# A fused attention and feed-forward kernel: each engine's issue order taken from a table in the source, in place of priorities and hand-set order

## Chip, cores and metric

The kernel runs on one core of one Trainium2 chip. The metric is the time of one execution on the device in microseconds (us); lower is better. The core has five instruction streams that run beside each other: TensorE (PE in the profile), VectorE (DVE), ScalarE (ACT), GpSimd (POOL) and SyncE (SP), which here only issues transfers. Each stream runs its instructions in the order in which they stand in it, and an instruction starts when what it waits for is done.

## The reference

Batch 4, 8 heads, 576 positions, head width 64, with a bias on the scores from a small network on the distance of two positions; then a feed-forward layer over 2304 tokens (model width 512, hidden width 2048).

```python
scores = q @ k.T / sqrt(64)
x      = log1p(|i - j|) / log1p(max(i, 1))          # one number for each pair of positions
bias   = relu(x * w1 + b1) @ w2                     # 32 hidden units, one value for each head
attn   = softmax(scores + bias)
a      = attn @ v                                   # heads side by side: 2304 x 512
h      = a @ w_in
g      = h * clip(h + 3, 0, 6) / 6
out    = g @ w_out
```

`w_in` and `w_out` arrive as 64-bit numbers (two 32-bit words each), and most products are made of three matmuls on 16-bit high and low parts (high by high, high by low, low by high).

## The kernel before

**Stages.** (1) The bias table: for 36 groups of 16 positions a hidden layer (`z_e` on DVE, `z_a` or `z_e` on ACT), a matmul (`b_ps`), an eviction with scale (`bo`, line 932 on ACT) and a store to DRAM. The attention tiles read the table back as `bt` or, for a tile that is used often, `k` (line 500, on SP). (2) `w_in` comes in 8 chunks of 1 MB: a load (line 248 on SP, into `w`), absolute value (258 on ACT), sign (259 on POOL), three DVE passes that put the two words together and take the row maximum (266, 269, 272), then a power-of-two scale of the row (210, 165, 215) and a split into a 16-bit high half (129 on ACT) and low half (146 on DVE, `wi`). Lines 266 to 272 write into the space of `wo`, the later home of `w_out`, so the first `w_out` loads can't start until the last low halves of `w_in` have been read from there. (3) `w_out` goes the same way in 8 chunks `cu`, staged in `wo` or `z_e`; the low halves are again line 146, into `wo`. The maximum over all its rows (line 152 `m_w`, a matmul `m_ps` on PE, line 161 `p_w`, then 220 and 222) gives `r_w2c`, with which the first hidden tiles `g` are scaled on DVE (line 127) before the first output matmul may read them. (4) `v_scale`: the maximum of |v| of each batch, from loads `va` or `vf` (line 179, SP) and a DVE reduction each (181). (5) 144 attention tiles: scores `s_ps` on PE, bias and row maximum on DVE (571, 750 ns each), the exponential on ACT (582), transposes `t_ps`, and the product with v `pv_ps`. (6) The feed-forward of each half batch: `h_ps` (line 793, PE), activation on ACT (783, 770), DVE (776) and POOL (772), `o_ps` (line 816, PE).

**What sets the order.** The program is traced by Python generators: the attention tiles go on one by one, and between them run steps of the weight preparation, the bias table and the feed-forward, at rates from a table of settings (`rw1`, `ro`, `rf` and others). A scheduler then places the traced instructions by a simulated timeline and by priorities (`ahead`, `low`, `ranked`, with offsets such as `a_bo` -100). Three things bind it further. `behind(k)` wraps many loads so that each comes after a bias load that was noted in `bias_loads` (an order without a wait). `keep_order("PE")` in `open_steady` switches to the traced order on PE from tile 37 on, and `keep_order("SP")` does so for SP from tile 45 on.

Of the kernel before, what the change touches and what calls it, by code (L numbers as in the profile page):

```python
# [13 lines left out]
U32 = mybir.dt.uint32  # L14
# [16 lines left out]
F64_BIAS = 2.0 ** -112  # L31
F64_MAX = float(np.uint32(0x0FEFFFFF).view(np.float32))


@with_exitstack
def attention_moe_kernel(
# [17 lines left out]
    nc = tc.nc  # L54
# [173 lines left out]

    bias_loads = []

    def behind(k=-1):

        return tc.issue_after(bias_loads[k]) if len(bias_loads) > max(k, 0) else nullcontext()

    def pick(name, k):
        return cfg[name][k % len(cfg[name])]

    def f64_load(src, k=None):

# [7 lines left out]
        with behind(cfg["wb"]) if k is not None else nullcontext():  # L247
            dq("w").dma_start(out=t, in_=src.bitcast(U32))
        return t
# [140 lines left out]
    def load_direct(b, p):  # L390

        t = qk_p.tile([128, 512 + S], F32, tag="hi", name="qk0")
        with behind():
            dq("q").dma_start(out=t, in_=qkd[b, p])
        qk_t[b, p, 0] = t
# [5 lines left out]
    def load_qk(b, p, u):  # L401
        w = S + QW[u]
        t = st_p.tile([128, 1024], F32, tag="st", name="st")[:, 0:w]
        with behind():
            dq("k").dma_start(out=t, in_=qk[b, p][:, 256 * u:256 * u + w])
        st_t[b, p, u] = t
# [34 lines left out]
    def load_v(b, p, u):  # L441
# [4 lines left out]
        else:  # L446
            t = st_p.tile([128, VC], F32, tag="vs", bufs=2, name="vs")
        with behind():
            dq("v").dma_start(out=t, in_=vp[b, p])
        v_t[b, p, u] = t  # L450
# [24 lines left out]
    def load_bias(b, p, i):  # L475
# [22 lines left out]
        else:  # L498
# [3 lines left out]
            )  # L502
        bias_loads.append(d.ins)
        return out, src
# [685 lines left out]
    HOLD, LAST = cfg['hold'], NT + 5  # L1190
    in_order = ctx.enter_context(ExitStack())

    def keep_order(*names):
        engines = {getattr(mybir.EngineType, e) for e in names}
        in_order.enter_context(tc.manual_schedule(engines=engines))


# [28 lines left out]
    def open_steady():  # L1226
# [8 lines left out]
        steady[0] = True  # L1235
        keep_order("PE")

# [33 lines left out]
    for n in range(-1, NT + 7):  # L1271
# [33 lines left out]
    for q_ in queue:  # L1305
        drain(q_)
    in_order.close()

# [60 lines left out]
```

## Time and profile before

| what | value |
|---|---|
| time, median of 3 runs | 670.89 us (667.25, 670.89, 673.08) |
| profiled execution | 668.28 us, span of the core 666.3 us |
| mean granted TensorE clock | 0.982 of full |
| busy: PE, DVE, ACT, POOL | 631.3, 462.4, 503.0, 212.6 us |

The span runs from the first to the last instruction of the core; the profiled execution's own time has 2 us around it. Matmuls are pipelined and their ends are modelled, so a busy share of 95% says that PE had little idle time, not that every matmul ran at its best rate. Times in the rows are in us from the span's start unless marked ns.

### The profile page before, as it was taken

To read this page: it belongs to the slowest core of one execution; us is meant where nothing else is said; L and a number is where in the kernel's file an instruction comes from. 1 tells how busy PE (TensorE), PEld (TensorE's weight loads), DVE (VectorE), ACT (ScalarE), POOL (GpSimd) and SP (SyncE) were. 2 spreads that over 40 slices of the span, in tenths; PEclk is the share of its full clock that TensorE was granted. 3 is DMA by queue.
4 is the path that set the end of the run, shared out by engine and by line. 5 is a ranking of instruction groups with operands and counts; after the bars stand their busy time and mean duration, and the time that the engine had idled before them with its cause. 6 is when DMAs were issued, how large, how long until landed. Compare 5 with 4: busy or idle time off the path is not lost.

```text
span 666.3 us, 14803 instructions
## 1 busy us (share of the span) xinstructions
PE 631.3 (95%) x5440; PEld 451.8 (68%) x5440; DVE 462.4 (69%) x1116; ACT 503.0 (75%) x993; POOL 212.6 (32%) x267
## 2 busy tenths in 40 slices
PE   8677899887999899999999999999999999999997
PEld 3224556664777667788888887777777777777775
DVE  6798978899866987867678676776687657731310
ACT  7996777887859998888689778876888678832620
POOL 0211124766121531154135314531244125300410
PEclk9977999998899999999999999999999999999999
DMA  8798967744688989998999999798979996550000
GB/s 294 281 347 301 372 251 265 246 177 149 178 204 203 234 209 260 235 211 208 286 253 217 252 220 179 142 203 183 184 134 197 183 193 127 97 102 21 1 11 31
DMA packets 176649, 130.58 MB, mean 196 GB/s; under 512 B 138304, under 2 KB 145728, under 8 KB 175552
## 3 DMA queue, kind: packets, MB, share of 16 engines
q1 hardware_dynamic: 166784, 114.14, 69.8%
q10 hardware_dynamic: 9792, 15.49, 7.9%
q8 instruction: 43, 0.70, 0.4%
q14 instruction: 30, 0.25, 0.1%
HBM read 77.54 MB, written 15.49 MB: 140 GB/s over the span
## 4 chain that ended last, share of the span: by engine, by line
PE 72%; DVE 9%; DMA 7%; issue 4%; ACT 3%; POOL 1%; ACTq 0%; SPq 0%; DVEq 0%; POOLq 0%
PE o_ps L816 28%; PE h_ps L793 24%; PE s_ps L559 9%; PE pv_ps L724 7%; DMA wo<-in_w_out_dram 3%; DMA va<-in_vp_dram 2%; PE b_ps L893 2%; DMA w<-in_w_in_dram 2%; DVE bt L571 1%; DVE cu L269 1%; DVE wo L272 1%; DVE wo L269 1%; DVE cu L272 1%; DVE cu L266 1%; DVE vparts L181 1%
## 5 line engine op out<-in xcount | busy, mean ns | idle before, releaser
L793 PE MATMUL h_ps<-x,wi 128*128 128x256 f16 (+1 forms) x1536 | 199.8, 288 | 1.7 <-DVE p_v L161 1.7
L816 PE MATMUL o_ps<-g,wo 128*128 128x256 f16 (+1 forms) x1536 | 196.5, 286 | 0.0
L793 PEld LDWEIGHTS <-wi 128*128 128x128 f16 x1536 | 148.4, 99 | 49.6 <-issue 11.1
L816 PEld LDWEIGHTS <-wo 128*128 128x128 f16 x1536 | 146.9, 98 | 46.8 <-issue 9.3
L772 POOL TENSOR_TENSOR g<-t,g 128x256 f16<-128x256 f32 (+1 forms) x128 | 105.5, 834 | 191.8 <-ACT g L770 191.0
L582 ACT ACTIVATE bt<-bt,sm 128x576 f32<-128x576 f32 x144 | 110.7, 770 | 39.7 <-DVE sm L571 38.0
L146 DVE SCALAR_TENSOR_TENSOR hl<-bt,sm,hl 128x576 f16<-128x576 f32 x112 | 95.5, 868 | 24.2 <-ACT hl L129 22.3
L129 ACT ACTIVATE hl<-bt,sm 128x576 f16<-128x576 f32 x112 | 83.9, 766 | 4.8 <-ACT bt L582 3.3
L776 DVE SCALAR_TENSOR_TENSOR t<-t,t,h_ps 128x320 f32<-128x320 f32 (+1 forms) x112 | 57.0, 515 | 38.9 <-ACT t L783 38.0
L418 POOL TENSOR_TENSOR qkl<-st,qkh 128x576 fp32r<-128x576 f32 (+2 forms) x48 | 55.8, 1184 | 72.7 <-ACT qkh L411 67.9
L770 ACT ACTIVATE g<-t 128x256 f16<-128x256 f32 (+1 forms) x128 | 55.3, 438 | 22.5 <-DVE t L776 22.1
L783 ACT ACTIVATE t<-h_ps,t,hr 128x320 f32<-128x320 f32 (+1 forms) x112 | 64.8, 587 | 9.2 <-PE h_ps L793 6.8
L571 DVE CUSTOM_DVE_ANT_0 bt<-s_ps,bt 128x576 f32<-128x576 f32 x88 | 64.6, 750 | 5.9 <-PE s_ps L559 4.2
L590 DVE TENSOR_SCALAR sm<-sm 128x1 f32<-128x1 f32 x112 | 16.7, 151 | 42.5 <-ACT bt L582 42.4
L826 ACT ACTIVATE ot<-o_ps,os 128x256 f32<-128x256 f32 (+1 forms) x32 | 15.7, 491 | 37.2 <-PE o_ps L816 34.8
L932 ACT ACTIVATE bo<-b_ps,cv_sb,isc 128x576 f32<-128x576 f32 (+36 forms) x60 | 36.0, 637 | 2.2 <-PE b_ps L893 2.0
L872 DVE TENSOR_SCALAR z_e<-T,nbp 128x576 f32<-128x576 f32 (+17 forms) x76 | 33.1, 486 | 4.4 <-PE b_ps L893 2.4
L571 DVE CUSTOM_DVE_ANT_0 bt<-s_ps,k 128x576 f32<-128x576 f32 x40 | 28.7, 751 | 8.3 <-PE s_ps L559 6.1
L724 PE MATMUL pv_ps<-at,vh 128*64 128x320 f16 (+1 forms) x432 | 32.0, 293 | 0.0
L259 POOL TENSOR_SCALAR w<-w 128x1024 f32<-128x1024 f32 x8 | 10.1, 1260 | 67.1 <-ACT wo L258 59.2
L539 PE MATMUL s_ps<-qk 64*128 64x288 f32 x128 | 25.5, 476 | 5.9 <-DVE sm L571 4.4
L876 ACT ACTIVATE z_e<-T,bp 128x576 f32<-128x576 f32 (+17 forms) x36 | 24.5, 703 | 7.8 <-PE b_ps L893 3.5
(130 smaller groups left out, 835.7 us busy)
## 6 DMA issues: line engine op xcount, KB each, us to landing
bt<-bias SPq DMA_DIRECT2D x36, 576.0 KB, 5.5
w<-in_w_in_dram SPq DMA_DIRECT2D x8, 1024.0 KB, 7.4
vs<-in_vp_dram SPq DMA_DIRECT2D x24, 320.0 KB, 4.5
st<-in_qk_dram SPq DMA_DIRECT2D x16, 448.0 KB, 4.1
bias<-bo ACTq DMA_DIRECT2D x20, 295.5 KB, 4.7
wo<-in_w_out_dram SPq DMA_DIRECT2D x5, 1024.0 KB, 5.8
bias<-bo ACTq DMA_DIRECT2D x16, 288.0 KB, 5.9
bt<-bias SPq DMA_DIRECT2D x32, 144.0 KB, 3.4
```

Source lines behind the costliest of these rows:

```text
L129: nc.scalar.activation(out=out, in_=full, func=AF.Copy, scale=scale)
L146: nc.vector.scalar_tensor_tensor(out=out, in0=full, scalar=scale, in1=high, op0=ALU.mult, op1=ALU.subtract)
L418: nc.gpsimd.tensor_sub(out=lo[:, c:c + w], in0=t[:, c:c + w], in1=hi[:, c:c + w].bitcast(F32))
L559: nc.tensor.matmul(out=s_t[n + j][:, a, 0:HALF], lhsT=w[q], rhs=m[rows, cs], start=(k == 0), stop=(k == 2),)
L571: nc.vector.tensor_tensor_reduce(out=halves(bt), in0=ps, in1=halves(src), op0=ALU.add, op1=ALU.min, scale=-0.125, scalar=3.0e38, accum_out ...
L582: nc.scalar.activation(out=bt, in_=bt, func=AF.Exp, scale=-1.0, bias=sm[:, 0:1], accum_out=total)
L724: nc.tensor.matmul(out=ps[64 * s:64 * s + 64, 0:n], lhsT=w[:, 128 * c + 64 * s:128 * c + 64 * s + 64], rhs=at[:, c, s * n:(s + 1) * n], st ...
L772: e.tensor_sub(out=g[:, 1], in0=uu, in1=g[:, 0])
L776: nc.vector.scalar_tensor_tensor(out=t_t[f], in0=t_t[f], scalar=cols(f)[2], in1=h_t.pop(f)[:, 0:n], op0=ALU.min, op1=ALU.mult,)
L783: nc.scalar.activation(out=t_t[f], in_=h_t[f][:, 0:n], func=AF.Relu, scale=cols(f)[0], bias=cols(f)[1],)
L793: nc.tensor.matmul(out=h_t[f][:, 0:n], lhsT=wi[:, a, c, f * 128:(f + 1) * 128], rhs=x[:, e, c], start=(k == 0), stop=(k == 3 * KC - 1),)
L816: nc.tensor.matmul(out=ops[:, 0:n], lhsT=wo[:, a, f, e * 128:(e + 1) * 128], rhs=g_t[f][:, r], start=(f == 0 and a == 0 and r == 0), stop= ...
```

## The change

The instructions and the data they pass stay as they were. `behind`, `bias_loads` and `keep_order` go. A table `ISSUE` gives for each engine a permutation of its traced instructions: SP 116 entries, POOL 247, ACT 907, DVE 939, PE 1367 (instructions by the number at which they are traced; whatever comes behind the last entry follows in traced order). At the end of the program `issue_in_order` adds, along each engine's list, a dependency from each instruction to the one before it that has no semaphore: it binds the scheduler's order on that engine and adds no wait. The priorities stay in the code, and the chain leaves them nothing to choose.

```diff
+ISSUE = {
+    "SP": """
+0-1 3 2 15 4 7 18 5 8 20 10 23 22 6 11 9 25 12-14 17 31 16 19 21 26 24 27 33 30 28 35 29 47 32 34 36
...
+    "DVE": """
+8 3 5-6 17 14 0 7 15 9-10 16 19 18 4 47 20 11 21 62 22 53 24 64-65 25 23 26 29 31 30 32 27-28 35
...
+def issue_in_order(tc, nc):
+
+    traced = {}
+    for i in nc.cur_bb.bb.instructions:
+        if not i.opcode.startswith("Tile"):
+            traced.setdefault(i.engine.name, []).append(i)
+    after = mybir.DependencyInfo(mybir.DependencyClass.NoSync, mybir.DependencyReason.DATA)
+    for name, seq in traced.items():
+        order = []
+        for run in ISSUE[name].split():
+            lo, _, hi = run.partition("-")
+            order.extend(range(int(lo), int(hi or lo) + 1))
+        order.extend(range(len(order), len(seq)))
+        for a, b in zip(order, order[1:]):
+            tc.add_manual_dep(seq[b], seq[a].name, after, reason="order")
...
-            with behind():
-                dq("v").dma_start(out=t, in_=vp[b, p])
+            dq("v").dma_start(out=t, in_=vp[b, p])
...
-    bias_loads = []
-
-    def behind(k=-1):
-
-        return tc.issue_after(bias_loads[k]) if len(bias_loads) > max(k, 0) else nullcontext()
...
-        steady[0] = True
-        keep_order("PE")
+        steady[0] = True
...
-        if n == cfg["spn"]:
-            keep_order("SP")
...
-    in_order.close()
+    issue_in_order(tc, nc)
```

Against the order before, every engine's instructions stand in another order up to a point and in the same one from there: PE in its first 1366 of some 5000 matmuls, DVE and ACT up to the places that the trace of before has at 256 us and shortly after 250 us, SP in its first 115 transfers. Three places follow. Numbers behind a name tell the tiles of one name apart; "x3" stands for three alike in a row. Line numbers of the kernel after are higher by some 149 for the same code up to line 460 and by some 137 below.

DVE at the end of the `w_out` preparation, before: `L161` is `p_w`, `L222` is `r_w2c`, `L146` on `wo` a low half of a chunk, `L146` on `hl` a low half of an attention tile, `L872` the hidden layer of the bias table.

```order
L872 TENSOR_SCALAR z_e_114<-T_113,nbp_117 128x320 x3
L594 RECIPROCAL sm_1588<-sm_1588 128x1
L594 RECIPROCAL sm_1654<-sm_1654 128x1
L161 TENSOR_REDUCE p_w2_1697<-m_ps_1695 128x1
L146 SCALAR_TENSOR_TENSOR wo_96<-cu_1626,w2s_1058,wo_96 128x1024
L203 TENSOR_SCALAR os0_1773<-hs0_991,p_w2_1697 128x1
L203 TENSOR_SCALAR os1_2169<-hs1_2165,p_w2_1697 128x1
L220 RECIPROCAL rm_w2_1699<-p_w2_1697 128x1
L203 TENSOR_SCALAR os2_3369<-hs2_3365,p_w2_1697 128x1
L146 SCALAR_TENSOR_TENSOR hl_1672<-bt_1306,sm_1588,hl_1672 128x576
L146 SCALAR_TENSOR_TENSOR hl_1733<-bt_1306,sm_1654,hl_1733 128x576
L222 TENSOR_SCALAR r_w2c_1701<-w2p_1057,rm_w2_1699 128x8
```

The same place after (`L310` is 161, `L368` and `L370` are 220 and 222, `L413` is 272, `L1009` is 872, `L276` is 127):

```order
L310 TENSOR_REDUCE p_w2_1697<-m_ps_1695 128x1
L731 RECIPROCAL sm_1588<-sm_1588 128x1
L368 RECIPROCAL rm_w2_1699<-p_w2_1697 128x1
L370 TENSOR_SCALAR r_w2c_1701<-w2p_1057,rm_w2_1699 128x8
L413 SCALAR_TENSOR_TENSOR cu_1626<-z_e_114,cu_1626 128x1024
L1009 TENSOR_SCALAR z_e_114<-T_113,nbp_117 128x320 x2
L276 TENSOR_SCALAR g_1353<-g_1353,r_w2c_1701 128x2x256
L727 TENSOR_SCALAR sm_1654<-sm_1654 128x1
L1009 TENSOR_SCALAR z_e_114<-T_113,nbp_117 128x320
L731 RECIPROCAL sm_1654<-sm_1654 128x1
L295 SCALAR_TENSOR_TENSOR hl_1672<-bt_1306,sm_1588,hl_1672 128x576
```

The chain of the maximum has moved ahead of the last packing pass, the hidden layer, the two `hl` halves and the low halves of the last two chunks (`cu_1564` and `cu_1626`); those two low halves stand 16 and 19 rows below the end of this piece.

DVE at the end of the `w_in` preparation, before: `L272` is the last packing pass, the two `L146` the low halves of the last two chunks.

```order
L272 SCALAR_TENSOR_TENSOR wo_96<-w64_628,wo_96 128x1024
L187 RECIPROCAL s_v1_697<-p_v1_694 128x1
L215 RECIPROCAL w1s_175<-w1p_174 128x1
L152 TENSOR_REDUCE m_w1_882<-w1p_174 128x1
L571 ISA bt_648,sm_806<-s_ps_766,bt_648 128x576
L571 ISA sm_806 128x1
L709 TENSOR_TENSOR xr_741<-pv_ps_715,xr_741 128x256
L146 SCALAR_TENSOR_TENSOR wi_95<-wo_96,w1s_175,wi_95 128x1024 x2
```

And after (`L413` is 272, `L295` is 146, `L708` is 571, `L301` is 152):

```order
L413 SCALAR_TENSOR_TENSOR wo_96<-w64_628,wo_96 128x1024
L295 SCALAR_TENSOR_TENSOR wi_95<-wo_96,w1s_175,wi_95 128x1024
L708 ISA bt_648,sm_806<-s_ps_766,bt_648 128x576
L708 ISA sm_806 128x1
L301 TENSOR_REDUCE m_w1_882<-w1p_174 128x1
L295 SCALAR_TENSOR_TENSOR wi_95<-wo_96,w1s_175,wi_95 128x1024
L846 TENSOR_TENSOR xr_741<-pv_ps_715,xr_741 128x256
```

The low halves of the last two chunks now follow the last packing pass more closely; the low halves of the two chunks before them, which stood at rows 93 and 89 of DVE, now come behind these.

SP at the loads of v for the maximum (`va`, line 179), before: `va_961` and `va_1022` stand behind the third load of `w_out`, and `va_1054` and `va_1089` behind the fourth.

```order
L248 DMA wo_96<-in_w_out_dram 128x2x1024
L500 DMA bt_941<-bias0_97 128x2x576
L449 DMA vf_958<-in_vp_dram 128x640
L394 DMA qk0_956<-in_qkd_dram 128x1088
L179 DMA va_961<-in_vp_dram 128x640
L179 DMA va_1022<-in_vp_dram 128x640
L500 DMA bt_1024<-bias128_98 128x2x576
L248 DMA wo_96<-in_w_out_dram 128x2x1024
L179 DMA va_1054<-in_vp_dram 128x640
L179 DMA va_1089<-in_vp_dram 128x640
```

And after, further up in SP's list (`L327` is 179, `L389` is 248, `L638` is 500):

```order
L327 DMA va_961<-in_vp_dram 128x640
L389 DMA w64_628<-in_w_in_dram 128x2048
L638 DMA bt_648<-bias0_97 128x2x576
L638 DMA bt_699<-bias128_98 128x2x576
L389 DMA z_e_114<-in_w_out_dram 128x2x1024
L327 DMA va_1022<-in_vp_dram 128x640
L638 DMA bt_759<-bias0_97 128x2x576
L389 DMA wo_96<-in_w_out_dram 128x2x1024 x2
```

`va_961` has moved ahead of the last load of `w_in`, and `va_1022` ahead of the first two loads of `w_out` into `wo`; `va_1054` and `va_1089` come behind the third of these and ahead of the fourth.

## Rows read from the trace of the kernel before

**Rows 1.** The page: busy us of each engine, its share of the span and its instructions.

```profile
PE 631.3 (95%) x5440; PEld 451.8 (68%) x5440; DVE 462.4 (69%) x1116; ACT 503.0 (75%) x993; POOL 212.6 (32%) x267
```

**Rows 2.** Windows: stretch, length, then PE, PEld, DVE, ACT, POOL, clock, DMA share, GB/s.

```profile
0.00:172.00 172.00, 142.30 (x1021) 81.63 (x1021) 147.81 (x325) 136.41 (x233) 57.74 (x54) 0.93 0.73 261
150.00:175.00 25.00, 21.13 (x136) 14.25 (x134) 24.43 (x65) 19.78 (x38) 10.60 (x10) 0.80 0.46 130
172.00:225.00 53.00, 51.20 (x489) 38.36 (x486) 37.73 (x105) 44.45 (x92) 13.75 (x16) 1.00 0.88 220
225.00:600.00 375.00, 375.00 (x3463) 286.89 (x3462) 267.56 (x671) 302.18 (x632) 128.46 (x182) 1.00 0.92 194
600.00:666.30 66.30, 62.79 (x475) 44.88 (x473) 9.30 (x17) 19.98 (x39) 12.64 (x16) 1.00 0.05 16
```

**Rows 3.** Critical chain, pieces from 85 to 97 us: start, us, what it ran or waited on.

```profile
85.22 1.29 DVE wi L146
86.53 7.50 DMA wo<-in_w_out_dram
94.11 1.15 ACT cu L258
95.28 1.33 DVE cu L266 x3
```

**Rows 4.** Waits of DVE, 0 to 172 us: total, times, longest.

```profile
DVE cu L266 <- ACT cu L258: 3.2, 2, 3.0
...
DVE vparts L181 <- DMA va<-in_vp_dram: 2.3, 1, 2.3
DVE bt L571 <- DMA k<-bias: 2.2, 1, 2.2
```

**Rows 5.** Timeline of DVE, 156 to 173 us: start, us, operation, wait before it.

```profile
157.99 1.88 DVE L146 SCALAR_TENSOR_TENSOR wo<-cu,w2s,wo 128x1024 f16<-128x1024 f32 x1
...
163.29 0.88 DVE L146 SCALAR_TENSOR_TENSOR vl<-vs,s_v,vh 128x640 f16<-128x640 f32 x1
...
164.43 1.21 DVE L272 SCALAR_TENSOR_TENSOR cu<-z_e,cu 128x1024 uint32<-128x1024 uint32 x1
...
165.88 1.07 DVE L872 TENSOR_SCALAR z_e<-T,nbp 128x320 f32<-128x320 f32 x3
...
167.77 1.27 DVE L146 SCALAR_TENSOR_TENSOR wo<-cu,w2s,wo 128x1024 f16<-128x1024 f32 x1
...
169.39 1.54 DVE L146 SCALAR_TENSOR_TENSOR hl<-bt,sm,hl 128x576 f16<-128x576 f32 x2
170.85 0.22 DVE L222 TENSOR_SCALAR r_w2c<-w2p,rm_w 128x8 f32<-128x8 f32 x1
```

**Rows 6.** Timeline of PE, 158 to 185 us, same columns.

```profile
162.75 1.53 PE L637 MATMUL t_ps<-eye_sb,bt 128*128 128x128 f32 x10 [3.16 <-DVE sm L571]
...
167.32 2.77 PE L793 MATMUL h_ps<-x,wi 128*128 128x256 f16 x12
...
172.04 0.50 PE L816 MATMUL o_ps<-g,wo 128*128 128x256 f16 x3
...
172.92 3.11 PE L816 MATMUL o_ps<-g,wo 128*128 128x256 f16 x27
...
176.95 2.14 PE L816 MATMUL o_ps<-g,wo 128*128 128x256 f16 x18
```

**Rows 7.** Waits of PE, 0 to 260 us.

```profile
PE s_ps L536 <- ACT bo L932: 4.8, 1, 4.8
...
PE h_ps L793 <- DVE p_v L161: 1.7, 1, 1.7
```

**Rows 8.** Timeline of SP, 60 to 125 us: start of issue, us, transfer.

```profile
65.29 0.92 SPq L248 DMA_DIRECT2D w<-in_w_in_dram  x1
...
85.33 1.56 SPq L248 DMA_DIRECT2D wo<-in_w_out_dram  x2
...
115.07 2.19 SPq L179 DMA_DIRECT2D va<-in_vp_dram  x2
```

More of the change, by code (lines that the diff above doesn't have):

```diff
@@ L1 @@
-from contextlib import ExitStack, contextmanager, nullcontext
+from contextlib import ExitStack, contextmanager
 from itertools import chain, count
@@ L32 @@
 F64_MAX = float(np.uint32(0x0FEFFFFF).view(np.float32))
+ISSUE = {
+    "SP": """
+0-1 3 2 15 4 7 18 5 8 20 10 23 22 6 11 9 25 12-14 17 31 16 19 21 26 24 27 33 30 28 35 29 47 32 34 36
+57 48 37 51 54 39 38 42 40 43 59 50 46 55 52 41 60 44-45 49 56 53 63 62 58 65 69 67 61 66 68 78
+75-76 64 70 73 72 80 77 79 83 82 74 86-87 71 90-91 81 94 89 85 88 100 96 84 101 92 97 99 93 102 98
+107 109 103 106 110 108 95 105 112 114-115 104 113 111
+""",
+    "Pool": """
+2-5 0 6-9 15 19 21 10 12-13 11 22 14 25 23 26 17 16 27 24 20 30 35 28 33 29 34 31 37 40 36 38-39 44
@@ new lines @@
+224-226 220 223 227 234-235 237-238 228-231 239 232-233 236 240-244 246 245
+""",
+    "Activation": """
+1 0 3-4 7-8 11 5 12 9 15 19 16 20 13 2 6 14 17 24 28 25 21 10 29 26 32 18 36 23 22 33 30 37 34 27 41
+31 42 38 40 46 35 43 45 50 58 47 52 51 39 44 54 59 55 53 74 62 56 48 61 65-66 57 63-64 60 67-68 75
+70 49 71 80 69 72-73 81 77 76 78 82 79 85 83 86 84 87-89 92 94 93 99 91 102 90 96 95 101 100 108 97
+103 109 104 106-107 113 111 110 137 146 117 112 114 105 98 115 118-119 116 151 120 125 121 123 122
@@ new lines @@
+897-898 900 899 902 901 904 903 906 905
+""",
+    "DVE": """
+8 3 5-6 17 14 0 7 15 9-10 16 19 18 4 47 20 11 21 62 22 53 24 64-65 25 23 26 29 31 30 32 27-28 35
+33-34 36 66 37 12 40 44 41 38 42 39 43 86 55 46 45 49 56-57 51-52 50 69 48 70 54 58-59 73 13 61
+74-75 60 68 71 63 76 72 82 2 67 83 81 84 87 79-80 88 85 89-90 95 94 97 96 98 91 99 101 100 104 92
+108 102 119 122 77 93 103 105 109 112 78 115-116 123 110 121 117 113-114 126 125 133 129 118 127 124
+128 106 131 120 153 107 143-144 111 137 132 138 130 139 135 172 175 173-174 176-177 134 136 152 155
@@ new lines @@
+817 821-823 827-829 834 826 832-833 838 830 835-837 840-841 847 842 831 846 839 843-845 849-851 856
+848 854-855 852 857 860 858-859 864-865 872 853 866 871 861-863 868-870 876-877 867 878 884 873-875
+882-883 879 890 880 887 885 888-889 894-895 902 896 881 901 886 891-893 898-900 906-907 897 908 914
+903-905 912-913 909 920 915 910 917-919 922-923 929 924 911 928 916 921 925-927 931-933 937 930
+935-936 938 934
+""",
+    "PE": """
+0-8 12 9-10 13-14 11 15-17 20 18-19 21-24 28 25 29-31 26 32 27 36-37 33-34 38-42 35 44 43 52 45-47
@@ new lines @@
+1261 1290-1292 1262-1263 1293-1302 1304-1307 1303 1308-1329 1332-1339 1341 1340 1342-1353 1330
+1354-1366 1331
+""",
+}
+def issue_in_order(tc, nc):
[12 more added lines that the diff above has]
+            tc.add_manual_dep(seq[b], seq[a].name, after, reason="order")
@@ L246, in f64_load @@
             t = wo[:, :, c:c + 4, :].rearrange("p a k e -> p a (k e)").bitcast(U32)
-        with behind(cfg["wb"]) if k is not None else nullcontext():
-            dq("w").dma_start(out=t, in_=src.bitcast(U32))
+        dq("w").dma_start(out=t, in_=src.bitcast(U32))
         return t
@@ L392, in load_direct @@
         t = qk_p.tile([128, 512 + S], F32, tag="hi", name="qk0")
-        with behind():
-            dq("q").dma_start(out=t, in_=qkd[b, p])
+        dq("q").dma_start(out=t, in_=qkd[b, p])
         qk_t[b, p, 0] = t
@@ L403, in load_qk @@
         t = st_p.tile([128, 1024], F32, tag="st", name="st")[:, 0:w]
-        with behind():
-            dq("k").dma_start(out=t, in_=qk[b, p][:, 256 * u:256 * u + w])
+        dq("k").dma_start(out=t, in_=qk[b, p][:, 256 * u:256 * u + w])
         st_t[b, p, u] = t
@@ L447, in load_v @@
             t = st_p.tile([128, VC], F32, tag="vs", bufs=2, name="vs")
-        with behind():
-            dq("v").dma_start(out=t, in_=vp[b, p])
+        dq("v").dma_start(out=t, in_=vp[b, p])
         v_t[b, p, u] = t
@@ L502, in load_bias @@
             )
-        bias_loads.append(d.ins)
         return out, src
@@ L1190, in attention_moe_kernel @@
     HOLD, LAST = cfg['hold'], NT + 5
[L1191 to L1195, printed above, removed]
     def open_ffn():
```

93 lines of the change are left out of this document (added).

## The prediction

> **What bounds the kernel now.** The page's first part comes first: PE is busy 631.3 of 666.3 us [rows 1], so at most some 35 us can be won without taking work from PE. The windows say where these are. Up to 172 us PE works 142.3 us, so 29.7 us are lost there; from 172 to 225 us it is 1.8; from 225 to 600 us nothing at all; behind 600 us 3.5 [rows 2]. A new order can win only in the opening, where the weights and the bias table are prepared and the first attention tiles run. From 225 us on PE is the bound, its work is the same, and from about 260 us on all orders are the same too, so whatever the opening wins or loses is passed through to the end almost unchanged.
>
> In the opening no engine is full: DVE works 147.8 of 172 us, ACT 136.4 and PE 142.3 [rows 2]. DVE is the nearest to full, 24.43 of 25 us from 150 to 175 us [rows 2], and the chain of waits runs over it again and again: the low half of a `w_in` chunk on DVE, a `w_out` load of 7.5 us that could not start before that, its first step on ACT, DVE again [rows 3]. So the end of the opening is DVE's work plus 24.2 us of DVE's own waits. What ends the opening is read on PE: the output matmuls `o_ps` start at 172.04 us, in groups of 3, 27 and 18, which is 48, one half batch's first tile (16 hidden chunks by three products) [rows 6]. Before them PE waits and runs at half clock: 12 `h_ps` take 2.77 us [rows 6], 231 ns each, and the granted clock is 0.80 in that window against 1.00 in the next [rows 2].
>
> **The change part by part.** It removes no operation and adds none, and the new dependencies carry no semaphore; the cost is in position alone.
>
> *The chain of the `w_out` maximum.* `r_w2c` is ready at 170.85 us [rows 5], `g` is then scaled, and `o_ps` starts 1.2 us later. The new order puts this chain ahead of the low half of chunk 6 (1.88), the low half of v (0.88), the last packing pass (1.21), the hidden layer (1.07), the low half of chunk 7 (1.27) and the two `hl` halves (1.54) [rows 5]. That is 7.9 us of DVE's work which used to stand ahead of `r_w2c`. The first `o_ps` could so start 7.9 us earlier, if nothing else holds it.
>
> *What is late next.* The two low halves of `w_out` are read by the last `o_ps` of the same tile: each chunk holds two of the 16 hidden chunks, so the last one is needed from the 43rd matmul of the 48 on. In the kernel before that one runs at 176.95 + 12 x 0.119 = 178.4 us (18 matmuls took 2.14 us [rows 6]). I summed, over DVE's instructions in the new order with their durations from this trace, what stands ahead of that low half: 150.9 us, against 144.7 in the old order. With DVE's waits as before (24.3 us up to there) it starts at 175.2 us and takes 1.27 [rows 5], so it ends at 176.5. That gate lets PE's `o_ps` move by 178.4 - 176.5 = 1.9 us only, and by one more us for each us that DVE waits less. So the second gate, not the first, sets the gain: 1.9 us plus what DVE's waits lose.
>
> *The low halves of `w_in`.* The two that free the space for the first `w_out` loads have 3.9 and 3.1 us less work ahead of them (again summed over the instructions), because two others were put behind them. The loads were issued at 85.33 us and later [rows 8], and DVE later stood 3.0 us, waiting for ACT's first step on the loaded chunk [rows 4]. Bounds of what is won: 0, if the loads are held by something else, and 3.0, the whole wait. The loads come 3 us earlier by the count, so I take 3.0.
>
> *The loads of v.* DVE waited 2.3 us for `va` [rows 4], issued at 115.07 us [rows 8] behind the fourth load of `w_out`; the new order has them ahead of it. Bounds: 0 and 2.3; I take 2.3, since the issue moves past a load that itself waited for a DVE pass. In return these loads stand ahead of weight loads: `va_961` waits for a buffer until DVE has reduced an earlier `va`, which the new order does right behind the packing pass that had let the last `w_in` load go at 65.29 us [rows 8]. It costs that load one reduction, about 0.8 us, hidden under the 3 us of the previous point.
>
> *The bias table.* DVE waits 2.2 us for the bias tile `k` [rows 4]. That tile comes from stores by ACT behind the table's groups, and the new order gives DVE 1.9 us less work ahead of this place, while ACT's work ahead of it is about the same. So DVE comes earlier and waits longer: minus 1.9. Bounds: 0 to 1.9 lost.
>
> *Other stalls.* PE's 4.8 us on `bo` [rows 7] lie where ACT makes the bias table; that PE wait is not on DVE's path, and I give it nothing. The 1.7 us that `h_ps` waits for `p_v` [rows 7] stay too: DVE has 3.1 us less work ahead of it, but PE comes earlier by as much and more. Bounds 0 and 1.7.
>
> *The sum.* DVE's waits lose 3.0 + 2.3 - 1.9 = 3.4 us; with the 1.9 of the second gate this is 5.3 us. The half clock can give back at most 1.4 us, half of the 2.77 [rows 6]; I leave it out. So 668.28 - 5.3 = 663.0 us for the profiled execution. The median of the three runs stands 670.89 / 668.28 = 1.0039 above it, which makes 665.6 us. The bounds of the terms: 1.9 + (0 + 0 - 1.9) = 0 and 1.9 + 3.0 + 2.3 + 1.7 + 1.4 = 10.3, or 670.9 and 660.6 us.
>
> *A rule against it.* The DMA engines were busy 0.73 of the time up to 172 us [rows 2], so there is room for a load to come forward. The Trainium skill ("DMA: Bandwidth & Descriptors", "Issuing engines are not separate DMA queues") says that transfers of all issuing engines run on the same 16 DMA engines and interleave; by that a load that comes forward takes from those beside it, and the 2.3 us of `va` would be paid by the weights, so that the sum would be 3.0 in place of 5.3. The row with its 0.73 leaves the room.
>
> **The rivals.** *The waits go almost altogether.* If a better order took half of DVE's 24.2 us of waits in the opening, 12 us, the second gate would move by 1.9 + 12 = 13.9 us, to 654.4, or 657 us on the median. For it speaks that the order is moved throughout, on five engines at once, and that PE has 29.7 us of idle time to give; against it, that I find only three named waits of 2 us and more whose cause the new order touches.
>
> *Given back.* Behind the opening PE is held by ACT: from 172 to 225 us ACT is busy 44.45 of 53 us, and DMA 0.88 [rows 2]. If PE comes to these earlier than they can follow, new waits eat the 5 us, and the result is 0 to -2 us: 669 to 671. For it speaks the wait on `p_v`; against it that PE has nothing to wait for from 225 us on, with DVE and ACT busy 0.71 and 0.81 of that stretch [rows 2].
>
> *Slower.* The second gate closes on PE. PE issues in order, so an `o_ps` that waits for the low half also holds the scores behind it, for which DVE waits in turn. In the new order the low halves stand behind three softmax steps and most of the `g` scalings, each of which may wait on POOL, ACT or PE. The point from which it decides is 1.9 us of added DVE waits; with 6 us of them PE stands 4 us, and if the clock falls as it did before 172 us, 48 `o_ps` at half clock take 5.75 us more (3 in 0.50, 27 in 3.11, 18 in 2.14 [rows 6]): 668.28 + 4 + 5.75 = 678, or 681 us. The rows show the half clock behind a wait of PE in just this place [rows 2, 6]; the Trainium skill ("TensorE: Matmul & The Clock Gate", "What's actually happening") says that the clock stands at half by default and is raised by activity of the array, with which this trace agrees. Against it speaks that the fixed order leaves the three softmax steps at places that PE's own order reaches earlier.
>
> *The table does not do what it says* (the scheduler keeps its own order): the instructions stand otherwise in the compiled order, so this has no chance worth counting.
>
> **How the numbers follow.** The forecast, 3 to 8 us won (663 to 668), has 0.42; waits gone almost altogether (654 to 663) 0.30; given back (668 to 673) 0.15; slower (above 674) 0.13. Three runs of before spread over 5.8 us, so 1%, 6.7 us, is about what a measurement of this kernel can tell from none. Faster than 664.2 us is the second case with a little under a third of the first: 0.43. Within 1% are the rest of the first and the third: 0.43. Slower than 677.6: 0.14, the last case and a remainder. The range leaves out some 0.08 at either end: 656 to 675 us.
>
> **What would show it.** Right: on PE, the first `o_ps` at 165 to 168 us in place of 172, a shorter wait or none ahead of it, and no wait of `o_ps` for `wo`; on DVE `r_w2c` at 161 to 165, the low halves of `wo` ending 2 us or less ahead of the `o_ps` that read them; the waits for ACT's first step and for `va` gone, and the wait for the bias tile `k` at about 4 us. From 260 us on the same stretch of work, shifted. Wrong: a wait of `o_ps` on DVE's line of the low halves, a clock under 0.9 behind 165 us, new waits of PE between 172 and 260 us, or a weight load that SP issues later than before.

## The result

| | before | after |
|---|---|---|
| median of 20 runs | 669.65 us (666.71 to 673.22) | 664.86 us (658.05 to 668.86) |
| ratio after to before | | 0.9908, 95% interval 0.9882 to 0.9933 |
| profiled execution | 668.28 us, span 666.3 | 661.57 us, span 659.5 |

The kernel became 0.9% faster; the forecast was 665.6 us. PE is still the engine that sets the time. The page of the kernel after, its line for PE, as in [rows 1]:

```profile
PE 630.1 (96%) x5440; PEld 451.0 (68%) x5440; DVE 463.1 (70%) x1116; ACT 505.3 (77%) x993; POOL 202.9 (31%) x267
```

The instructions are the same in number; PE's busy time moved by 1.2 us, and the span by 6.8. The windows of the kernel after say where these 6.8 us come from (columns as in [rows 2]):

```profile
0.00:164.00 164.00, 144.30 (x1075) 85.45 (x1076) 150.69 (x332) 141.10 (x239) 48.14 (x51) 0.96 0.76 273
0.00:172.00 172.00, 152.30 (x1146) 90.77 (x1147) 156.24 (x350) 148.54 (x254) 51.10 (x54) 0.96 0.76 269
150.00:175.00 25.00, 23.98 (x205) 17.20 (x206) 22.39 (x66) 23.94 (x45) 6.01 (x7) 1.00 0.46 117
172.00:225.00 53.00, 51.43 (x495) 38.15 (x493) 39.59 (x106) 45.01 (x96) 15.91 (x23) 1.00 0.95 228
225.00:300.00 75.00, 70.32 (x704) 52.88 (x702) 52.95 (x135) 62.56 (x130) 22.83 (x31) 1.00 1.01 229
```

Count the matmuls rather than the busy time, since a matmul at half clock is busy for twice as long and does no more (12 `h_ps` took 2.77 us at half clock and 27 `o_ps` of the same shape 3.11 us at full clock [rows 6]). By 172 us PE has done 1146 where it had done 1021, and by 225 us another 6 more. From 225 to 300 us it does 704, and the kernel before did 759 there, without a pause:

```profile
225.00:300.00 75.00, 75.00 (x759) 56.94 (x758) 57.21 (x145) 66.70 (x143) 25.14 (x35) 1.00 1.03 227
```

That is the kernel before, and it also gives the price of one matmul, 75.00 / 759 = 0.0988 us. So the new order is 125 matmuls or 12.4 us ahead at 172 us, gains 0.6 to 225 us, and gives 55 matmuls or 5.4 us back by 300 us. The sum is 7.6, against 6.8 of the span; one mean price for unlike matmuls makes this an estimate. Read at the same work instead, the first `o_ps` comes 14.2 us earlier (157.80 against 172.04, below), and 6.8 us are left at the end, so 7.4 us are given back. **Both halves of this are larger than the forecast, and they offset each other.**

**The opening.** Waits of DVE up to 172 us, after:

```profile
DVE bt L708 <- DMA k<-bias: 3.2, 1, 3.2
...
DVE wo L407 <- ACT wo L399: 1.4, 2, 0.7
```

Of [rows 4] the 2.3 us for `va` are gone, and the 3.0 on ACT's first step as well (the 1.4 here are the same step of other chunks). The wait for the bias tile `k` grew from 2.2 to 3.2. What came of it stands in the timelines. DVE:

```profile
153.80 0.23 DVE L370 TENSOR_SCALAR r_w2c<-w2p,rm_w 128x8 f32<-128x8 f32 x1
...
162.47 1.27 DVE L295 SCALAR_TENSOR_TENSOR wo<-cu,w2s,wo 128x1024 f16<-128x1024 f32 x1
...
164.51 1.28 DVE L295 SCALAR_TENSOR_TENSOR wo<-cu,w2s,wo 128x1024 f16<-128x1024 f32 x1
```

and PE:

```profile
157.80 1.91 PE L953 MATMUL o_ps<-g,wo 128*128 128x256 f16 x16
...
165.90 0.83 PE L953 MATMUL o_ps<-g,wo 128*128 128x256 f16 x6
```

`r_w2c` comes at 153.80 in place of 170.85, the first `o_ps` at 157.80 in place of 172.04. The last low half of `w_out` ends at 164.51 + 1.28 = 165.79, and the last six `o_ps` begin at 165.90. The loop takes the high half twice and then the low half, so the third of these six is the first that reads it, at some 166.1 us. PE shows no wait there; three engines are full at this place:

```profile
153.00:166.00 13.00, 12.92 (x107) 9.28 (x106) 12.85 (x37) 13.00 (x26) 2.17 (x2) 1.00 0.47 121
```

PE (12.92 of 13.00 us) thus comes to the second gate just after it has opened; that the gate holds PE is not shown. ACT (13.00) scales 8 of the 16 tiles `g` here, as it does in the kernel before; the description of the stages named DVE alone. The clock stands at 1.00 in the window from 150 to 175 us, where [rows 2] had 0.80: PE goes from one work to the next and no longer stops ahead of `o_ps`.

**Behind it.** ACT is stopped by a transposing transfer (`hl` into `at`, issued by SP). The chain of waits of the kernel after, two pieces of it:

```profile
248.29 7.06 DMA bt<-bias
255.37 9.66 DMA at<-hl
```

ACT's timeline where that transfer lands:

```profile
265.14 0.77 ACT L278 ACTIVATE hl<-bt,sm 128x576 f16<-128x576 f32 x1 [3.03 <-DMA at<-hl]
...
267.82 0.77 ACT L1013 ACTIVATE z_e<-T,bp 128x576 f32<-128x576 f32 x1
```

SP issues the transposing transfer at 255.37 us, 0.02 us after a `bt` load has landed that it issued 7.06 us before; the transfer then takes 9.66 us and holds the `hl` buffer that ACT has to write next. ACT issues in order: the hidden layer `z_e` of the bias table stands behind that, and PE waits for it. PE's longest waits from 172 to 300 us, of which [rows 7] shows only the 1.7 us for `p_v` in the kernel before:

```profile
PE b_ps L1030 <- ACT z_e L1013: 2.5, 1, 2.5
PE pv_ps L861 <- DMA vh<-vh: 1.4, 1, 1.4
```

Such transfers are not slower than before. From 225 to 300 us those from `hl` into `at` take 3.2 to 9.7 us from issue to landing in both kernels (median 6.3 before, 6.6 after), and in the kernel before ACT waits for none of them.

### The profile page after: what moved, and what is told of

It reads as the page before. It is cut to its first block, busy times and chain, and to the rows that moved or that the text cites. A ratio compares the mean times of both kernels' runs of the same rounds, so it can differ in the third digit from the quotient of the medians.

```text
span 659.5 us, 14782 instructions
## 1 busy us (share of the span) xinstructions
PE 630.1 (96%) x5440; PEld 451.0 (68%) x5440; DVE 463.1 (70%) x1116; ACT 505.3 (77%) x993; POOL 202.9 (31%) x267
## 4 chain that ended last, share of the span: by engine, by line
PE 58%; DMA 6%; ACT 2%; POOL 1%; issue 1%; SPq 1%; ACTq 0%; DVE 0%; POOLq 0%
PE o_ps L953 23%; PE h_ps L930 22%; PE s_ps L696 7%; PE pv_ps L861 6%; DMA at<-hl 3%; DMA bias<-bo 2%; DMA bt<-bias 1%; DMA vh<-vh 1%; ACT hl L278 1%; ACT bo L1069 1%; POOL g L909 0%; ACT bt L719 0%; ACTq L1083 0%; SPq L601 0%; ACT g L907 0%
## 5 line engine op out<-in xcount | busy, mean ns | idle before, releaser
L930 PE MATMUL h_ps<-x,wi 128*128 128x256 f16 (+1 forms) x1536 | 204.8, 286 | 2.2 <-DVE t L913 1.2
L953 PE MATMUL o_ps<-g,wo 128*128 128x256 f16 (+1 forms) x1536 | 198.6, 286 | 0.0
L930 PEld LDWEIGHTS <-wi 128*128 128x128 f16 x1536 | 146.6, 98 | 52.5 <-issue 16.4
L909 POOL TENSOR_TENSOR g<-t,g 128x256 f16<-128x256 f32 (+1 forms) x128 | 102.0, 807 | 194.9 <-ACT g L907 186.5
L295 DVE SCALAR_TENSOR_TENSOR hl<-bt,sm,hl 128x576 f16<-128x576 f32 x112 | 94.7, 857 | 24.2 <-ACT hl L278 22.2
L557 POOL TENSOR_TENSOR qkl<-st,qkh 128x576 fp32r<-128x576 f32 (+2 forms) x48 | 54.4, 1151 | 69.3 <-ACT qkh L550 64.2
L708 DVE CUSTOM_DVE_ANT_0 bt<-s_ps,bt 128x576 f32<-128x576 f32 x88 | 64.9, 749 | 7.3 <-PE s_ps L696 6.4
L1009 DVE TENSOR_SCALAR z_e<-T,nbp 128x576 f32<-128x576 f32 (+17 forms) x76 | 35.6, 491 | 3.7 <-PE b_ps L1030 1.9
L708 DVE CUSTOM_DVE_ANT_0 bt<-s_ps,k 128x576 f32<-128x576 f32 x40 | 28.7, 751 | 8.6 <-PE s_ps L696 5.4
L774 PE MATMUL t_ps<-eye_sb,bt 128*128 128x128 f32 x160 | 30.4, 286 | 1.2 <-ACT atf L777 0.8
L861 PEld LDWEIGHTS <-vh 128*64 128x64 f16 x432 | 22.2, 109 | 9.6 <-issue 5.0
```

Of the source, the lines that this page charges most:

```text
L295: nc.vector.scalar_tensor_tensor(out=out, in0=full, scalar=scale, in1=high, op0=ALU.mult, op1=ALU.subtract)
L557: nc.gpsimd.tensor_sub(out=lo[:, c:c + w], in0=t[:, c:c + w], in1=hi[:, c:c + w].bitcast(F32))
L708: nc.vector.tensor_tensor_reduce(out=halves(bt), in0=ps, in1=halves(src), op0=ALU.add, op1=ALU.min, scale=-0.125, scalar=3.0e38, accum_out ...
L861: nc.tensor.matmul(out=ps[64 * s:64 * s + 64, 0:n], lhsT=w[:, 128 * c + 64 * s:128 * c + 64 * s + 64], rhs=at[:, c, s * n:(s + 1) * n], st ...
L909: e.tensor_sub(out=g[:, 1], in0=uu, in1=g[:, 0])
L930: nc.tensor.matmul(out=h_t[f][:, 0:n], lhsT=wi[:, a, c, f * 128:(f + 1) * 128], rhs=x[:, e, c], start=(k == 0), stop=(k == 3 * KC - 1),)
```

## The experiments

Two questions were open: what in the order wins 12 us in the opening where 5.3 were expected, and what takes 5 us back. For the second there are two theories. **A:** PE now comes early to a stretch that transfers and buffers limit (the DMA share is 1.01 there), so part of any win is taken back; this may sit in the `hl` buffers (A1) or in the transfers' speed (A2). **B:** the order itself is worse behind the opening, whenever PE gets there. Ratios are to the kernel before on the same chip, with 95% intervals. Where an edit says "order of before", the numbers in the table are those that the scheduler had chosen, written into `ISSUE`.

**The table with the old order.**

```diff
 ISSUE = {
-    "SP": order of after ...
+    "SP": order of before ...            (all five engines)
```

> The table holds the order of the kernel before (read out of its compiled program), with behind and keep_order gone: the way of the change without its order. If only the order counts, this is the kernel before: ratio 1.00 within 0.3%, first o_ps at 172 us, PE without idle time from 225 us on. If the table as such (other semaphores, no priorities) costs or wins something, it shows here as a ratio off 1.00.

668.80 us, ratio 0.9976 (0.9945 to 1.0007), first `o_ps` at 171.52 us, and PE busy 74.98 us from 225 to 300. The table as such costs nothing that this resolves; the time comes from the order that it holds.

**The new opening with the old tail, and the other way round.** The first takes the order of after for all that had started by 157.8 us, and the order of before for the rest. The second keeps the order of before up to the first `o_ps` and takes that of after behind it.

```diff
-ISSUE: order of after
+ISSUE: order of after up to 157.8 us, the rest in the order of before       (first)
+ISSUE: order of before up to 172 us, the rest in the order of after         (second)
```

> Everything that the kernel after starts before 157.8 us (its first o_ps) in the new order, all behind it in the order of before. Theory A, the 14 us won in the opening are taken back from 200 to 280 us because the transfers of that stretch take their time in any order: o_ps starts at 158 us and the time is that of the kernel after, ratio 0.988 to 0.994. Theory B, the new order of the tail is what loses them: with the old tail most of the 14 us stay, ratio 0.980 or below.

> The reverse: the order of before up to its first o_ps at 172 us, the new order behind it. Theory A: the opening costs what it did, o_ps starts at 172 us, and the tail has no idle time to give, ratio 0.998 to 1.002. Theory B: a bad tail shows here as a loss, ratio 1.005 to 1.01.

The first: 670.48 us, 0.9986 (0.9955 to 1.0018); nothing of the win is left, which neither theory expected. Its PE timeline, PE's longest wait up to 300 us, DVE's timeline ahead of the end of that wait, and a wait of DVE in the opening:

```profile
164.74 0.49 PE L936 MATMUL o_ps<-g,wo 128*128 128x256 f16 x3
173.19 4.93 PE L936 MATMUL o_ps<-g,wo 128*128 128x256 f16 x27
```

```profile
PE t_ps L757 <- DVE sm L691: 7.2, 2, 6.8
```

```profile
165.59 1.63 DVE L278 SCALAR_TENSOR_TENSOR wo<-cu,w2s,wo 128x1024 f16<-128x1024 f32 x1
...
169.30 1.28 DVE L278 SCALAR_TENSOR_TENSOR wo<-cu,w2s,wo 128x1024 f16<-128x1024 f32 x1 [1.14 <-ACT wo L261]
```

```profile
DVE bt L691 <- DMA bt<-bias: 4.7, 1, 4.7
```

Three `o_ps` go and the next come 8 us later. The opening wins its time by putting DVE work off (the low halves of `w_out` and of v); the old tail asks for it at once, and PE waits 6.8 us for the DVE softmax step behind it. Part of the loss lies elsewhere: DVE waited 4.7 us for a bias tile early in this execution, as in others with the new opening (further below), and its first `o_ps` stands at 164.74 and not at 157.80, close to that of the unchanged kernel with such a wait (165.31). The opening can't be judged without the tail that it was made for.

The second: 672.62 us, 1.0044 (1.0016 to 1.0071), so the new tail alone is a little slower. Its window:

```profile
225.00:300.00 75.00, 71.69 (x722) 53.22 (x720) 55.08 (x141) 65.34 (x139) 24.93 (x35) 1.00 1.02 240
```

PE comes to this stretch at the old time (first `o_ps` at 171.66 us) and loses 3.3 us of 75, with the same waits (ACT 2.5 us for `at`, PE 1.9 us for `z_e`). The table with the old order took 668.80 us on the same chip, and the two intervals do not touch, so the new tail behind the old opening costs some 3.8 us. That speaks for B.

**The first 86 us alone.**

```diff
-ISSUE: order of after
+ISSUE: order of after up to 86 us, the rest in the order of before
```

> New order for what the kernel after starts before 86 us (the w_in preparation, the early loads of v), the order of before behind it. In the trace of after the tiles near 86 us come 2.7 us earlier and the w_out loads 2 to 3 us. If each part of the opening wins by itself, o_ps starts 2.5 to 4 us earlier (168 to 169.5 us) and the time follows, ratio 0.994 to 0.997; if the parts need one another (the old order behind it waits again), nothing is left, ratio 0.999 to 1.003.

679.56 us, 1.0144 (1.0110 to 1.0179), first `o_ps` at 183.21 us: slower by 1.4% where a gain was expected. Two waits of 4 us and more appear on DVE, one of them 4.6 us for a bias tile,

```profile
DVE bt L682 <- DMA bt<-bias: 4.6, 1, 4.6
```

and the other 4.4 us for a step of POOL. The first is the wait that the unchanged kernel after has in some executions too (further below), so it need not come from the seam between the two orders. That the low halves that were put off fall due where the old order has no place for them is argued here, not shown. The gain that the prediction adds up by parts was not had by this part.

**Six `hl` buffers (A1), and a pad in the opening (A).**

```diff
-    hl_p = ctx.enter_context(tc.tile_pool(name="hl", bufs=5))
+    hl_p = ctx.enter_context(tc.tile_pool(name="hl", bufs=6))
-        t = st_p.tile([128, 1024], F32, tag="st", name="st")[:, 0:w]
+        t = st_p.tile([128, 896], F32, tag="st", name="st")[:, 0:w]
```

```diff
+    pad = const.tile([128, 2], F32, name="pad")
+    nc.vector.memset(pad, 0.0)
+    for _ in range(4):
+        nc.vector.tensor_reduce(out=pad[:, 1:2], in_=pad[:, 0:1].to_broadcast([128, 1024]), op=ALU.max, axis=AX.X)
```

The narrower `st` tile makes room for the buffer; the pad stands in DVE's list ahead of the tail.

> The kernel after with six buffers in place of five in the pool that the attention tiles' halves (hl), the bias rows (bo) and xr share; the space comes from two load buffers that are 512 B longer than any load into them. In the kernel after ACT stands 3.0 us at 262 us and 1.0 us at 231 us for a buffer that a transposing transfer holds, and PE then 2.5 us for ACT. Theory A1, ACT's order and the buffers hold the stretch from 200 to 280 us: these waits go and the time falls by 2 to 4 us, ratio to before 0.984 to 0.988. Theory A2, the transfers themselves hold it: another wait takes the place, ratio as the kernel after, 0.989 to 0.993.

> The kernel after with four reductions of 1024 elements more on DVE (about 1.1 us each, on a pad of their own) just ahead of the w_out maximum: the opening made some 4.5 us longer on its critical engine. If the stretch behind the opening is held by transfers (A1, A2), o_ps starts at 161 to 162.5 us but the time rises by 0 to 1.5 us, ratio 0.991 to 0.993. If the opening is passed through to the end, the time rises by all of it, ratio 0.997 to 0.999.

Six buffers: 668.80 us, 1.0008 (0.9978 to 1.0038), worse than the kernel after itself and outside both expected ranges. But its opening was another: DVE waited 4.1 us for a bias tile in it, and the first `o_ps` came at 170.98 us. Taken alone it decides nothing on A1. The pad: 674.69 us, 1.0059 (1.0026 to 1.0091), also worse than either range, first `o_ps` at 174.77 us. Its DVE timeline and its window:

```profile
160.65 4.98 DVE L1438 TENSOR_REDUCE pad<-pad 128x1 f32<-128x1024 f32 x4
```

```profile
225.00:300.00 75.00, 71.02 (x714) 52.69 (x711) 54.95 (x142) 64.29 (x135) 24.27 (x33) 1.00 1.03 249
```

Both kernels have such a wait for a bias tile in the opening (5.2 us here), but one has six buffers and the other five. The kernel after run again (further below) has the wait and five buffers, with its first `o_ps` at 165.31 us and a ratio of 0.9924. Against it the pad made the first `o_ps` 9.5 us later, which is more than its own 5.0 us and not explained, and the ratio 0.0135 higher, or 9.0 us of 669. And with PE later than in the kernel before, 4.0 us of the stretch are still lost. So where PE is late the length of the opening is passed on, and PE's early coming is not all that loses the stretch: A in its strong form is wrong.

**More transfers (A2).** Two copies of 1 MB from DRAM to DRAM, on SP, placed in the stretch; once in the kernel after, once in the order of before.

```diff
+    for j in range(2):
+        spare = dr_p.tile([64, 2 * DFF], F32, name=f"spare{j}")
+        nc.sync.dma_start(out=spare.bitcast(U32), in_=w_in[0:64, :].bitcast(U32))
```

> The kernel after with two more transfers of 1 MB from DRAM to DRAM, issued by SP at its places of 222 and 245 us; nobody reads them. Theory A2, the 16 DMA engines are the bound of that stretch: the time rises by what the transfers take, 4 to 8 us, ratio 0.997 to 1.003. If they have room to spare: at most 1 us, ratio 0.991 to 0.993.

> The same two transfers in the order of before (given as a table), at SP's places of 236 and 259 us. PE has no idle time there and the DMA engines are busy 0.95 to 1.0 of the time. If PE alone is the bound, at most 1 us more, ratio 0.997 to 1.001; if the DMA engines are as close to being the bound as theory A2 has it, 3 to 7 us more, ratio 1.003 to 1.008.

In the order of before: 672.37 us, 1.0043 (1.0010 to 1.0076), and PE stays full, 75.00 us from 225 to 300 us. But this trace is of one of the fastest of its ten runs (668.72 us), and the time rose by 0.4%, which lies in the range of A2; where it goes, the trace does not show. In the kernel after: four runs between 664.77 and 676.68 us, too far apart for an interval. The one trace of it, of a run of 675.15 us, has PE busy 66.70 us of the 75, the least of all kernels. So A2 is left open on both sides; what is shown is one execution under the old order in which 2 MB more did not stop PE.

**The kernel after once more.** All five kernels above that begin in the order of after (old tail, first 86 us, six buffers, pad, more transfers) waited 4.1 to 5.2 us for a bias tile where the first profile of the kernel after shows no such wait. So the kernel after ran again, unchanged.

> The kernel after, unchanged. Three kernels with its order (five buffers made six, a pad, more transfers) all lost 4 to 5 us on DVE at 33 to 43 us, where the first bias tile bt came late, which the first profile of the kernel after didn't show. If the new order by itself runs both ways, some executions of this one lie at 658 to 662 us and others above 667, and the profile shows either DVE's wait for bt (4 to 5 us) or none. If the additions made it, the wait is absent and the ratio is 0.988 to 0.994.

665.05 us (658.78 to 670.80), 0.9924 (0.9895 to 0.9954); profiled 665.66 us. This execution has the wait:

```profile
DVE bt L708 <- DMA bt<-bias: 5.3, 1, 5.3
```

Its first `o_ps` comes at 165.31 us, not 157.80. The cause stands at 31 us. The store on ACT's queue in this run, and SP's timeline:

```profile
31.83 0.53 ACTq L1083 DMA_DIRECT2D bias<-bo  x1
```

```profile
31.61 0.33 SPq L389 DMA_DIRECT2D w<-in_w_in_dram  x1
...
38.53 2.12 SPq L638 DMA_DIRECT2D bt<-bias  x2
```

and the same two of the kernel after in its first profile:

```profile
30.46 0.53 ACTq L1083 DMA_DIRECT2D bias<-bo  x1
```

```profile
31.13 0.33 SPq L389 DMA_DIRECT2D w<-in_w_in_dram  x1
...
33.93 0.90 SPq L638 DMA_DIRECT2D bt<-bias  x2
```

The store is the last one (`bo_322`) of the table's first part, for which the first `bt` load waits. In the first profile it is issued 0.67 us ahead of a 1 MB load of `w_in`, and the `bt` load goes 3.5 us after it. In the second it is issued 0.22 us behind that load, and the `bt` load goes 6.7 us after it. In the five kernels above it is issued behind the load too, by 0.04 to 1.59 us. The same program falls on either side of a margin of less than one us; between these two executions the first `o_ps` differs by 7.5 us and the time by 4.1 (661.57 and 665.66). The twelve times of this run do not fall into two groups.

The end of the opening in this execution, its window up to 172 us, DVE's last low half and PE's last group of `o_ps`:

```profile
0.00:172.00 172.00, 146.20 (x1079) 85.10 (x1080) 150.39 (x332) 141.69 (x240) 48.80 (x51) 0.97 0.75 261
```

```profile
172.03 1.28 DVE L295 SCALAR_TENSOR_TENSOR wo<-cu,w2s,wo 128x1024 f16<-128x1024 f32 x1
```

```profile
173.43 0.83 PE L953 MATMUL o_ps<-g,wo 128*128 128x256 f16 x6
```

**The store put first.** In ACT's list the stores of `bo_290`, `bo_306` and `bo_322` go right behind the evictions that they store. Around the last of them, without the other two:

```diff
  L1069 ACTIVATE bo_322
+ L1083 DMA bias0<-bo_322
  L1013 ACTIVATE z_e x2
  L1069 ACTIVATE bo_338
  L399 ACTIVATE wo<-w64_275
  L1013 ACTIVATE z_a
- L1083 DMA bias0<-bo_322
```

> The kernel after with three transfers moved on ACT's list: the stores of the last three bias rows of the first block stand right behind the evictions that fill them (in the new order the last of them stands 6 places behind, and behind ACT's first step on the third w_in chunk, which waits for its load). Theory F: the late store meets a w_in load of 1 MB on the rings and lands 3 us later in some executions, which holds the first bt. Then the store goes out near 28.7 us in place of 30.5 to 32.2, bt is issued by 33 us, DVE's wait for it is under 1 us, and the ratio is 0.984 to 0.991, with less spread than the kernel after. If the store isn't what holds bt, nothing changes.

662.05 us (658.95 to 663.45), 0.9902 (0.9873 to 0.9931); 8 of the 12 runs of the unchanged kernel beside it lie above its highest. The long wait is not there. Its store, and its `bt` load on SP:

```profile
29.37 0.53 ACTq L1083 DMA_DIRECT2D bias<-bo  x1
```

```profile
33.12 1.08 SPq L638 DMA_DIRECT2D bt<-bias  x2
```

The store leaves 1.7 us ahead of the load (31.09 us), the `bt` load goes 3.8 us after it, and the first `o_ps` comes at 159.38 us. The intervals of the two ratios overlap, so the size of the win isn't settled; that the place of this store sets the wait is. In all nine traces that begin in the order of after, the last section's included, the long wait is there where the store is issued behind the load and absent where it is issued ahead.

**The end of the `w_out` preparation alone.** The order of before, with only the chain of the maximum moved ahead and the two low halves put off, as in the first piece of order shown above.

```diff
-ISSUE: order of after
+ISSUE: order of before; on DVE 43 places, on PE 17 changed around r_w2c
```

> The order of before as a table, with one part of the change: at the end of the w_out preparation the chain of the maximum (152, 161, 220, 222 and its matmul on PE) goes ahead of the last packing pass, the hidden layer, the hl halves and the low half of v, and the low halves of the last two w_out chunks go behind the next softmax steps. By the prediction's two gates: r_w2c 6 to 8 us earlier (163 to 165 us), the first o_ps at 165 to 167, and the second gate (the last low half) lets 2 to 5 us through, ratio 0.993 to 0.997. If this part needs the rest of the table, PE waits in the middle of the o_ps and the ratio is 1.00.

672.95 us, 1.0074 (1.0046 to 1.0101): slower, which was not expected. DVE and PE in it:

```profile
161.10 0.23 DVE L338 TENSOR_SCALAR r_w2c<-w2p,rm_w 128x8 f32<-128x8 f32 x1
...
176.31 1.27 DVE L263 SCALAR_TENSOR_TENSOR wo<-cu,w2s,wo 128x1024 f16<-128x1024 f32 x1
```

```profile
168.26 0.50 PE L921 MATMUL o_ps<-g,wo 128*128 128x256 f16 x3
...
177.64 1.03 PE L921 MATMUL o_ps<-g,wo 128*128 128x256 f16 x4 [2.76 <-DVE sm L695]
```

The first `o_ps` comes 3.8 us earlier than in [rows 6], but the last low half ends at 177.58, and the last four `o_ps` wait 2.76 us and start at 177.64 (the row names the short DVE step that ends just behind the low half; no `o_ps` reads it). PE's clock is 0.86 from 150 to 175 us. This is the rival "slower" of the prediction: the second gate closes on PE when DVE does not get there earlier as a whole.

**Early store and six buffers.**

> The early stores and the six buffers of the shared pool together, so that the buffers are judged behind a good opening. In the run with the early stores ACT stood 4.3 us at 262 us for a buffer that a transposing transfer held (9.6 us from issue to landing), and PE 4.0 us for ACT behind it. Theory A1, one more buffer is what lacked: that wait goes, PE stays full from 225 to 300 us, ratio 0.984 to 0.987. Theory A2, the transfers of the stretch are too slow for PE's pace: PE still loses 3 to 5 us between 225 and 300 us, at another wait, ratio 0.988 to 0.992.

The edits are those of the two kernels above together. 659.31 us (656.94 to 664.19), 0.9869 (0.9830 to 0.9908): the best of all, and its interval lies below that of six buffers without the early store (0.9978 to 1.0038). Its window, and under it that of the early store alone:

```profile
225.00:300.00 75.00, 72.13 (x742) 55.79 (x739) 55.50 (x143) 65.26 (x138) 23.85 (x34) 1.00 1.07 243
```

```profile
225.00:300.00 75.00, 70.38 (x692) 53.07 (x691) 53.68 (x136) 61.88 (x131) 23.27 (x32) 0.98 0.98 229
```

With the buffer PE waits for `z_e` 1.3 us in place of 4.0, and does 742 matmuls in the stretch in place of 692. That is what A1 says of this wait. But it rests on one profile of each, six buffers in the other opening did 705, and the times of the two kernels overlap (0.9902 and 0.9869), so A1 is likely and not shown.

**What the stretch shows over all kernels.** From 225 to 300 us PE was busy 70.3 to 72.4 us in seven traces with the new tail (after, its second profile, old opening, six buffers, pad, early store, and both), wherever the first `o_ps` stood between 157.8 and 174.8 us, and 66.7 us with more transfers. Under the old tail it was 75.0 us in three traces and 73.2 to 73.9 in the three with a changed opening. These six do not differ in kind: in each PE waits 1.7 to 2.2 us for `p_v` [rows 7], and where PE is later the wait falls behind 225 us and so into the window.

So the order of the tail (B) costs time wherever PE stands: 3.8 us by the runs with the old opening. PE's early coming (A) seems to cost more on top: the two profiles of the kernel after are 7.5 us apart at the first `o_ps` and 4.1 in the time, so 3.4 us more were lost in the early one. The sixth buffer helped only there: with the first `o_ps` at 159 to 160 us it took the profiled time from 663.45 to 658.80 us, with PE late there is no such gain (672.24 us, against 672.44 with five buffers and the old opening). These are single executions, and runs of one kernel spread over 6 to 11 us, so B's share is shown and A's, with A1 as its likely form, is not. Which of the tail's moves costs the time stays open.

## Why the prediction was right

The time was 664.86 us against 665.6, and the direction and the range held. By its steps:

- **What bounds the kernel**: right that a new order could win only in the opening, and from about 280 us on both kernels run the same work, 6.8 us apart, to the end. Wrong that what the opening wins "is passed through to the end almost unchanged": of 14.2 us at the first `o_ps` 6.8 came through. That PE has nothing to wait for from 225 us on was true of the order before alone; the new one leaves 4.7 us of waits between 225 and 300 us.
- **The second gate sets the gain, 1.9 us plus what DVE's waits lose**: the sums hold, the wait at the gate is not seen. DVE's work ahead of the last low half was worked out as 150.9 us and is 151.2. The last group of `o_ps` begins at 165.90 us against 178.4, 12.5 us earlier; less 1.9, DVE's waits should have lost 10.6 us, and they went from 24.2 us (172 - 147.8, up to the old place) to 13.3 (164 - 150.7, up to the new one), 10.9 us. Since a place on DVE is always its work plus its waits, this agreement tests the 150.9 and little more; PE shows no wait at the gate. That the gate can close is shown by the kernel with the end of the preparation alone. There the last four `o_ps` wait, so the low half is needed from the 45th matmul on, not from the 43rd; that is 0.2 us.
- **DVE's waits lose 3.4 us**: in the first profile this term was mis-sized, it is 10.9. `va` (2.3) went as costed, with 0.6 on another load of v in its place; the step of ACT (3.0) went too; `k` cost 1.0 and not 1.9. The rest are waits of 1 to 2 us each, for which the prediction found no cause and counted nothing: on POOL's sign step, on the maximum's matmul, on the table's `b_ps`. Which move ended each of them no run shows. In the second profile of the same kernel the term is 2.6: DVE's waits are 21.6 us (172 - 150.4) up to the last low half, 5.3 of them for the bias tile, and the last group of `o_ps` begins at 173.43, 5.0 us earlier than 178.4. There the sum of the opening holds, and its first `o_ps` at 165.31 and `r_w2c` at 161.33 us lie where the prediction put them. That one late store decides between 2.6 and 10.9 the prediction did not see.
- **The half clock, 1.4 us left out**: it went altogether, 0.80 to 1.00. The 1.7 us for `p_v`, taken to stay, went too.
- **The rule against it**, with the 2.3 us of `va` paid by the weights: not seen in the first profile. The wait for `va` went, no wait for a weight load came in its place, and the DMA share up to 172 us is 0.76 against 0.73.
- **Given back**: the prediction held this and "the waits go almost altogether" as rivals to each other; both happened, one behind the other. By the count of matmuls 5.4 us of 12.4 were lost again, by the first `o_ps` 7.4 of 14.2, and new waits of PE between 172 and 260 us, one of its signs of being wrong, are there. So for the first profile the forecast of the time was good by luck: two errors offset each other, the larger gain and the new loss. In the second the opening won about what was forecast, and half of that was lost behind it (665.66 against 668.28).
- **Slower**: did not happen in the kernel after. Its mechanism is real: the kernel with the end of the preparation alone shows it.

## What to carry to other kernels

An order over five engines is one thing: pieces of a better order, put into the old one, were worth nothing or cost up to 1.4%, and the rows of two of them show the reason: they save time by putting off work for which only the rest has a place. (In the traces of two of the four the store comes late, which is part of their loss.) To say what an order is worth, count the bound engine's instructions by stage in both traces, and look for what the new order gives back behind the stage that it helps. And in a fixed order, look for a store or load whose place against a large transfer hangs on less than one us: here it went with 7.5 us at the first output matmul and 4.1 us in the time.

## What the hardware showed that was not expected

A store of 288 KB issued 0.2 us behind a 1 MB load on the other queue held up the load that waits for it for 6.7 us, and ahead of the load 3.5 to 3.8 us. The two queues were not separate roads. The Trainium skill ("DMA: Bandwidth & Descriptors", "Queues, rings and completion order") says that each DMA engine takes turns, packet by packet, between the queues that have work for it. The trace agrees in that the store beside the load is slowed: it took 6.6 us from issue to landing, and 3.3 when issued ahead. It does not show a fair share of the bytes, since the store of 288 KB landed 1.2 us later than the load of 1024 KB that it followed by 0.2 us; why, stays open.

A transposing transfer from `hl` into `at` took 9.66 us from issue to landing where the DMA share was 1.01, and 9.63 us in the kernel with the early store. It holds its source for that time. In the kernel before such transfers take up to 9.7 us too, and ACT waits for none of them: the order decides whether a slow transfer is a stop.
